# A linear-attention and MoE kernel: decay and bonus rows by the ScalarE queue, and the bonus rows turned ahead of unit 0's transposes

## Chip, cores and metric

One core of a Trainium2 chip. The metric is device time in microseconds of one execution; the median of five runs of the kernel before is 197.82 us (197.74 to 198.13).

## What is computed

The reference is a recurrent attention (RWKV-5 form) followed by a two-layer MLP with a SiLU between its layers. Batch 4, 8 heads, 768 steps, head size 48; the MLP is 384 to 2048 to 384 over all 3072 tokens.

```python
for t in range(S):
    kt, vt, rt = k[:, :, t], v[:, :, t], r[:, :, t]
    cur = np.einsum('bhd,bhe->bhde', u[None] * kt, vt)
    y[:, :, t] = np.einsum('bhd,bhde->bhe', rt, state + cur)
    state = w[None, :, :, None] * state + np.einsum('bhd,bhe->bhde', kt, vt)
...
h = x @ w_in                       # x: y with the heads side by side
out = (h * (1.0 / (1.0 + np.exp(-h)))) @ w_out
```

Two small inputs matter here: `w` (the decay, 8 x 48 numbers) and `u` (the bonus, 8 x 48 numbers).

## The kernel before

The sequence is cut into chunks of 128 steps. A unit is one chunk of one batch element; there are 24, taken chunk by chunk with the four batch elements inside. Unit i has its r, k and v as three loads of 192 KB each on the SP queue (`load`, L64), into six rotating buffers.

In a unit, TensorE transposes r and k of head pairs into PSUM (`p1`, L223), VectorE multiplies them by powers of the decay while it evacuates them (L226 for r, L230 for k), TensorE multiplies them into 128 x 128 score tiles (`p2`, L267 and L269), VectorE masks these (L276), and TensorE multiplies the masked scores with v (`p3y`, L293). The bonus term goes another way: GpSimd computes `ku` = k times u (`nat_ku`, L180) and `rku_f` = r times ku (`nat_rk`, L186), VectorE sums it per head (`bonus_sum`, L197), and ScalarE (unit 0, `bonus_act`, L211) or GpSimd (`bonus_vu`, L203) multiplies v by the sums. VectorE adds the two terms (`p3e`, L300), TensorE transposes the result (`p4`, L346), ScalarE evacuates it (L347), and the MLP's first layer follows (`l1`, L358), later its second (`l2`, L370). From the second chunk on a state is carried as well.

The order of instructions on every engine is the order of the program's text: the schedule is written out by hand from L426 on, and each engine works through its own list in order. MLP matmuls are put between the attention steps as fillers.

What precedes unit 0 is this. `w` and `u` come as rows of four partitions, 1.5 KB each (`load_row`, L84). SP's list starts with the decay row, then r and k of unit 0, the bonus row (handed in as `mid` at L89), v of unit 0, and the loads of units 1 to 3. ScalarE's list starts with a table load and a one-column SiLU (L116). TensorE starts with `spin(5)`, five matmuls on a zeroed tile that serve no result (L125); then `to_cols` turns the decay row into columns (L129), and four more spins follow (L139). From the decay's columns VectorE builds all powers up to 128 in seven doublings (L152 to L156); the tile of the powers is `pif`. Then comes `p1(0)`, with the r transposes, the k transposes, and in between the two evacuations, in the text at L227, the bonus row's turn: `to_cols_u` (L409) transposes it into columns (L129 again), ScalarE copies these (L134), four transposes of the broadcast columns spread them over 128 partitions (`to_rows`, L147), and ScalarE copies that into `u_bc` (L149).

GpSimd's list after its constants begins with a one-column copy that waits for r of unit 1 (`gate`, L434), the issue of the first quarter of the first MLP weight (`win_part(0, 512)`, L417), then `ku` of unit 0, which needs `u_bc`, `rku_f` of unit 0, and the same pair for unit 1, the second quarter's issue, and `vu` of unit 1.

VectorE's list after L230 of unit 0: the two masks of unit 0, L226 and L230 of unit 1, the bonus sums of units 0 and 1 (L197), the two masks of unit 1, and the two additions L300.

```python
    load_row(wrow, w)
    load(0, mid=lambda: load_row(urow, u))
...
    spin(5)
    wT = to_cols(wrow, None)
    spin(4)
...
    p1(0, mid=to_cols_u)
...
    nc.gpsimd.tensor_copy(out=gate, in_=rin[1][:, 0, 0:1])
    win_part(0, 512)
    nat_ku(0)
    nat_rk(0)
```

Of the kernel before, what the change touches and what calls it, by code (L numbers as in the profile page):

```python
# [15 lines left out]
def kernel(  # L16
# [11 lines left out]
    nc = tc.nc  # L28

    B, H, S, D = r.shape  # L30
# [5 lines left out]
    PR = 64 + D  # L36
# [16 lines left out]
    vin = [big.tile([128, H, D], FP, name=f"vin{i}") for i in range(NIN)]  # L53
# [7 lines left out]
    def unit(i):  # L61
        return divmod(i, B)

    def load(i, mid=None):  # L64
        if i >= NU:
            return
        sc, b = unit(i)
        for t, src in ((rin, r), (kin, k), (vin, v)):
            if t is vin and mid:
                mid()  # L70
            nc.sync.dma_start(out=t[i % NIN][:, :, 0:D],
                              in_=src[b, :, sc * C:sc * C + C, :]
                              .rearrange("h t d -> t h d"))
# [4 lines left out]
    urow = cst.tile([NP, 2, 64], FP)  # L78
# [3 lines left out]
        nc.vector.memset(t[:, :, D:64], 1.0)  # L82

    def load_row(t, src):  # L84
        nc.sync.dma_start(out=t[:, :, 0:D], in_=bass.AP(tensor=src.tensor, offset=0,
                                                        ap=[[PW, NP], [D, 2], [1, D]]))

    load_row(wrow, w)
    load(0, mid=lambda: load_row(urow, u))  # L89
    for i in range(1, B):  # L90
        load(i)
    for t in (rin, kin):
        nc.vector.memset(t[0][:, :, D:64], 0.0)
# [6 lines left out]
        out=maskM, in_=maskM, compare_op=ALU.is_ge, fill=0.0,  # L100
# [17 lines left out]
    def spin(n, t=None):  # L118

        if t is None:  # L120
            t = ps.tile([128, 512], FP, name="spin", tag="t", bufs=5)
        else:
            t = t.rearrange("s p t -> s (p t)")
        for _ in range(n):
            nc.tensor.matmul(t, junk[:, 0:128], junk, start=True, stop=True)  # L125

    def to_cols(row, copy):
        t = ps.tile([128, 512], FP, name="cols", tag="t", bufs=5)
        nc.tensor.transpose(t[0:PR, 0:NP], row.rearrange("p j d -> p (j d)")[:, 0:PR],  # L129
                            ident[0:NP, 0:NP])  # L130
        if copy is None:
            return t[0:PR, 0:NP]
        c = cst.tile([PR, NP], FP, name="cols_sb")
        copy(out=c, in_=t[0:PR, 0:NP])  # L134
        return c

    spin(5)
    wT = to_cols(wrow, None)
    spin(4)  # L139
    u_bc = cst.tile([128, H, D], FP)  # L140
    lamC = cst.tile([128, H, D], FP)

    def to_rows(dst, cols):

        t = ps.tile([128, NP, 2, 64], FP, name="rows", tag="t", bufs=5)
        for p in range(NP):
            nc.tensor.transpose(t[:, p, :, :].rearrange("t j d -> t (j d)")[:, 0:PR],  # L147
                                cols(p), ident[0:PR, 0:PR])
        nc.scalar.copy(out=dst.rearrange("t (p j) d -> t p j d", j=2), in_=t[:, :, :, 0:D])  # L149


    nc.vector.tensor_copy(out=pi[:, 0:NP, 1:2], in_=wT.unsqueeze(2))  # L152
# [2 lines left out]
    while n < C:  # L155
        nc.vector.tensor_tensor(  # L156
            out=pi[:, :, 1 + n:1 + 2 * n], in0=pi[:, :, 1:1 + n],
# [14 lines left out]
    def nat_v(i):  # L172
        L = live.setdefault(i, {})
        L["v16"] = wrk.tile([128, H, D], F16, name="v16", bufs=6)
        nc.scalar.copy(out=L["v16"], in_=vin[i % NIN])

    def nat_ku(i):
        L = live.setdefault(i, {})
        L["ku"] = wrk.tile([128, H, D], FP, name="ku")
        nc.gpsimd.tensor_tensor(out=L["ku"], in0=kin[i % NIN][:, :, 0:D], in1=u_bc,  # L180
                                op=ALU.mult)

    def nat_rk(i):
        L = live[i]
        L["rku_f"] = wrk.tile([128, H, D], FP, name="rku_f")
        nc.gpsimd.tensor_tensor(out=L["rku_f"], in0=rin[i % NIN][:, :, 0:D], in1=L["ku"],  # L186
                                op=ALU.mult)
# [23 lines left out]
            nc.scalar.activation(out=L["vu"][:, h, :], in_=vin[i % NIN][:, h, :],  # L211
                                 func=AF.Copy, scale=L["rku"][:, h:h + 1])

    def p1(i, mid=None, spins=0):
        n = i % NIN
        L = live.setdefault(i, {})
        tr = ps.tile([128, NP, C], FP, name="tr", tag="t", bufs=5)
        tk = ps.tile([128, NP, C], FP, name="tk", tag="t", bufs=5)
        spin(spins, tr)
        for t, src in ((tr, rin), (tk, kin)):  # L220
            flat = src[n].rearrange("p h d -> p (h d)")
            for p in range(NP):
                nc.tensor.transpose(t[0:PR, p, :], flat[:, 128 * p:128 * p + PR], ident)  # L223
        rk = wrk.tile([PR, 2, NP, C], FP, name="rk")
        L["rT"] = rk[:, 0]
        nc.vector.tensor_tensor(out=L["rT"], in0=tr[0:PR], in1=lamR, op=ALU.mult)  # L226
        if mid:  # L227
            mid()
        L["kT"] = rk[:, 1]
        nc.vector.tensor_tensor(out=L["kT"], in0=tk[0:PR], in1=lamK, op=ALU.mult)  # L230

# [174 lines left out]
            f()  # L406


    def to_cols_u():  # L409
        t = to_cols(urow, nc.scalar.copy)  # L410
        to_rows(u_bc, lambda p: t[:, p:p + 1].broadcast_to([PR, 128]))

    zero = junk[0:PR, 0:HD].rearrange("r (p c) -> r p c", p=NP)
    gate = cst.tile([128, 1], FP)

    def win_part(c0, c1):
        nc.gpsimd.dma_start(out=win[:, :, c0:c1],  # L417
                            in_=moe_w_in[:, c0:c1].rearrange("(q p) n -> p q n", p=128))
# [4 lines left out]
            in_=moe_w_out[1024 * g:1024 * g + 1024, :].rearrange("(f p) n -> p f n", p=128))  # L423


    p1(0, mid=to_cols_u)  # L426
    nat_v(0)
    lamCT = cst.tile([PR, NP, C], FP)
    for p in range(NP):
# [1 line left out]
                             scale=pi[:, p, C:C + 1])  # L431

    nc.scalar.copy(out=st[0], in_=zero)
    nc.gpsimd.tensor_copy(out=gate, in_=rin[1][:, 0, 0:1])  # L434
    win_part(0, 512)
    nat_ku(0)
    nat_rk(0)
    p2(0)
    p1(1, spins=1)
    bonus_sum(0)  # L440
    nat_ku(1)
    nat_rk(1)
    nat_v(1)
    p3y(0)
    to_rows(lamC, lambda p: lamCT[:, p, :])
    bonus_act(0)
    nc.scalar.copy(out=st[1], in_=zero)
# [8 lines left out]
    spin(1)  # L456
    p4(0)
    p1(2)
    nat_ku(2)
    nat_rk(2)  # L460
    nat_kc(0)
    win_part(1024, 1536)
    win_part(1536, 2048)
    nc.gpsimd.memset(rin[B][:, 0, 0:1], 0.0)
    load(B)
    load(B + 1)
    p4(1)
# [169 lines left out]
```

## Time and profile before

| what | value |
|---|---|
| median of five runs | 197.82 us |
| the profiled execution | 197.77 us |
| its span, first to last instruction | 196.1 us |
| outside the span | 1.7 us |
| TensorE busy | 189.6 us, 97% of the span |
| VectorE, ScalarE, GpSimd busy | 115.4, 90.9, 115.1 us |
| DMA, mean over the span | 123 GB/s |
| wait of L197 for GpSimd in the first 17 us | 0.8 us, once |

A profile has several views. The page gives busy shares and 40 slices of the span; the chain of waits follows the work that ended last back to its start; the timeline lists instructions with start and duration in us, and in brackets how long the engine was idle before and who ended that; the table by stretch gives busy time per engine in chosen windows. Matmul ends in these records are modelled, starts are measured. TensorE is busy nearly throughout, so that what its first useful matmuls wait for early in the span is paid in full, while the other engines' idle time mostly is not.

### The profile page before, as it was taken

To read this page: it belongs to the slowest core of one execution; us is meant where nothing else is said; L and a number is where in the kernel's file an instruction comes from. 1 tells how busy PE (TensorE), PEld (TensorE's weight loads), DVE (VectorE), ACT (ScalarE), POOL (GpSimd) and SP (SyncE) were. 2 spreads that over 40 slices of the span, in tenths; PEclk is the share of its full clock that TensorE was granted. 3 is DMA by queue.
4 is the path that set the end of the run, shared out by engine and by line. 5 is a ranking of instruction groups with operands and counts; after the bars stand their busy time and mean duration, and the time that the engine had idled before them with its cause. 6 is when DMAs were issued, how large, how long until landed. Compare 5 with 4: busy or idle time off the path is not lost.

```text
span 196.1 us, 4923 instructions
## 1 busy us (share of the span) xinstructions
PE 189.6 (97%) x1919; PEld 127.5 (65%) x1919; DVE 115.4 (59%) x233; ACT 90.9 (46%) x207; POOL 115.1 (59%) x145
## 2 busy tenths in 40 slices
PE   7989999999999999999999999999999999999993
PEld 2757878787767887675657656557656556644563
DVE  6687658885857774975486686467576344210121
ACT  3475487799212534216861125682025680069300
POOL 4499969979975779678668737835537710000000
PEclk9999999999999999999999999999999999999999
DMA  4999999999794783477456387616561011210022
GB/s 82 201 191 173 181 230 181 186 193 197 148 201 130 162 175 80 110 172 159 83 104 133 106 181 158 133 32 125 120 162 43 20 22 43 90 51 0 3 82 80
DMA packets 89696, 24.12 MB, mean 123 GB/s; under 512 B 82888, under 2 KB 89672, under 8 KB 89672
## 3 DMA queue, kind: packets, MB, share of 16 engines
q1 hardware_dynamic: 85992, 20.66, 48.7%
q0 software_dynamic: 3680, 3.15, 10.7%
q8 instruction: 15, 0.25, 0.5%
q14 instruction: 9, 0.07, 0.1%
HBM read 20.45 MB, written 4.72 MB: 128 GB/s over the span
## 4 chain that ended last, share of the span: by engine, by line
PE 87%; DVE 4%; issue 4%; POOL 3%; ACT 0%; POOLq 0%; DVEq 0%
PE ops L370 31%; PE hps L358 31%; PE ae L267 11%; PE xs L242 4%; PE y L293 3%; DVE am L276 2%; PE y L290 2%; PE sps L309 2%; PE ops L384 1%; POOL rku_f L186 1%; POOL ku L180 1%; PE yT L346 1%; PE ao L269 1%; DVE y L300 1%; DVE rku L197 1%
## 5 line engine op out<-in xcount | busy, mean ns | idle before, releaser
L361 ACT ACTIVATE gT<-hps 128x256 f16<-128x256 f32 (+1 forms) x128 | 59.7, 493 | 50.6 <-PE hps L358 48.9
L358 PE MATMUL hps<-xT,win 128*128 128x256 f16 (+1 forms) x384 | 69.2, 326 | 0.2
L370 PE MATMUL ops<-wout,gT 128*128 128x384 f16 x368 | 63.8, 326 | 0.0
L358 PEld LDWEIGHTS <-win 128*128 128x128 f16 x384 | 35.4, 98 | 22.9 <-issue 0.8
L370 PEld LDWEIGHTS <-gT 128*128 128x128 f16 x368 | 34.7, 98 | 22.4
L276 DVE TENSOR_TENSOR am<-ae,maskM 128x512 f16<-128x512 f32 x24 | 16.6, 691 | 33.4 <-PE ao L269 33.4
L374 DVE COPY osb<-ops 128x384 f32<-128x384 f32 x23 | 12.7, 553 | 28.8 <-PE ops L370 28.7
L267 PEld LDWEIGHTS ae<-rk 48*128 48x128 f32 x192 | 23.1, 187 | 7.6 <-issue 4.9
L267 PE MATMUL ae<-rk 48*128 48x128 f32 x192 | 27.7, 285 | 0.1
L269 PE MATMUL ao<-rk 48*128 48x128 f32 x192 | 27.7, 285 | 0.0
L203 POOL TENSOR_TENSOR vu<-vin,rku 128x384 f32<-128x384 f32 x23 | 19.1, 830 | 14.3 <-DVE rku L197 14.2
L259 ACT CAST rT<-rk 112x512 f16<-112x512 f32 x20 | 12.3, 615 | 31.7 <-DVE rk L253 31.7
L253 DVE TENSOR_TENSOR rk<-xs,pif 112x512 f32<-112x512 f32 x40 | 25.6, 680 | 1.7 <-PE xs L242 1.7
L180 POOL TENSOR_TENSOR ku<-kin,u_bc 128x384 f32<-128x384 f32 x24 | 24.1, 1006 | 1.9 <-DMA kin<-in_k_dram 1.9
L186 POOL TENSOR_TENSOR rku_f<-rin,ku 128x384 f32<-128x384 f32 x24 | 24.1, 1006 | 1.9
L191 POOL TENSOR_TENSOR kc<-kin,lamC 128x384 f16<-128x384 f32 x24 | 24.0, 1003 | 0.0
L269 PEld LDWEIGHTS ao<-rk 48*128 48x128 f32 x192 | 23.1, 187 | 0.0
L323 POOL CAST stb<-st 112x384 f16<-112x384 f32 x12 | 6.0, 503 | 20.4 <-DVE st L318 20.4
L300 DVE TENSOR_TENSOR y<-y,vu 128x384 f16<-128x384 f32 x24 | 13.4, 557 | 7.6 <-PE y L293 2.2
L276 DVE TENSOR_TENSOR am<-ao,maskM 128x512 f16<-128x512 f32 x24 | 16.3, 680 | 0.0
L197 DVE TENSOR_REDUCE rku<-rku_f 128x8 f32<-128x384 f32 x24 | 13.2, 549 | 2.0 <-POOL rku_f L186 1.6
L325 POOL TENSOR_TENSOR sdec<-st,pif 112x384 f32<-112x384 f32 x16 | 13.3, 836 | 1.1 <-ACT gT L361 1.1
(74 smaller groups left out, 170.0 us busy)
## 6 DMA issues: line engine op xcount, KB each, us to landing
rin<-in_r_dram SPq DMA_DIRECT2D x24, 192.0 KB, 2.8
kin<-in_k_dram SPq DMA_DIRECT2D x24, 192.0 KB, 3.4
vin<-in_v_dram SPq DMA_DIRECT2D x24, 192.0 KB, 3.7
out_dram<-osb SPq DMA_DIRECT2D x23, 192.0 KB, 1.9
win<-in_moe_w_in_dram POOLq DMA_DIRECT2D x4, 384.0 KB, 6.2
wout<-in_moe_w_out_dram POOLq DMA_DIRECT2D x2, 768.0 KB, 9.9
xT<-y SPq DMA_TRANSPOSE x18, 2.3
out_dram<-osh SPq DMA_DIRECT2D x1, 128.0 KB
```

The source lines that it names most:

```text
L180: nc.gpsimd.tensor_tensor(out=L["ku"], in0=kin[i % NIN][:, :, 0:D], in1=u_bc, op=ALU.mult)
L186: nc.gpsimd.tensor_tensor(out=L["rku_f"], in0=rin[i % NIN][:, :, 0:D], in1=L["ku"], op=ALU.mult)
L191: nc.gpsimd.tensor_tensor(out=kc[i % NKC][:, :, 0:D], in0=kin[n][:, :, 0:D], in1=lamC, op=ALU.mult)
L203: nc.gpsimd.tensor_tensor(out=L["vu"], in0=vin[i % NIN], in1=L["rku"].unsqueeze(2).broadcast_to([128, H, D]), op=ALU.mult)
L253: nc.vector.tensor_tensor(out=rk[:, :, :, 64 * g:64 * g + 64], in0=xs[g][0:PR], in1=lam(g), op=ALU.mult)
L267: nc.tensor.matmul(ae[:, p, :], L["kT"][0:D, p, :], L["rT"][0:D, p, :], start=True, stop=True)
L269: nc.tensor.matmul(ao[:, p, :], L["kT"][64:PR, p, :], L["rT"][64:PR, p, :], start=True, stop=True)
L276: nc.vector.tensor_tensor(out=am, in0=a, in1=maskM.unsqueeze(1).broadcast_to([128, NP, C]), op=ALU.mult)
L300: nc.vector.tensor_tensor(out=L["y16"], in0=L["y"], in1=L["vu"], op=ALU.add)
L358: nc.tensor.matmul(hps, win[:, q, ft * 128:(ft + 1) * 128], xts[sc][:, q, b0:b1, :].rearrange("p b t -> p (b t)"), start=(q == 0), stop=(q ...
L361: nc.scalar.activation(out=gts[sc][:, ft, b0 * C:b1 * C], in_=hps, func=AF.Silu)
L370: nc.tensor.matmul(ops, gts[sc][:, ft, b * C:(b + 1) * C], wout[:, ft, :], start=(ft == 0), stop=(ft == NFT - 1))
```

## The change

Three edits in the lead-in, all ahead of unit 0's scores.

- `load_row` issues on ScalarE's queue and no longer on SP's. ScalarE's list starts with the decay row and the bonus row, ahead of the table load. SP's list starts with r of unit 0; its order is otherwise the same.
- TensorE's list: six spins, the decay row's turn, one spin, the bonus row's turn, two spins, the four spreading transposes, and only then r and k of unit 0. There are nine spins as before. ScalarE's copies for the bonus keep their place in ScalarE's order. The argument `mid` goes.
- GpSimd's list: `ku` of unit 0 stands ahead of the gate and of the issue of the first weight quarter.

VectorE's order is unchanged.

```diff
-    def load(i, mid=None):
+    def load(i):
...
         for t, src in ((rin, r), (kin, k), (vin, v)):
-            if t is vin and mid:
-                mid()
             nc.sync.dma_start(out=t[i % NIN][:, :, 0:D],
...
     def load_row(t, src):
-        nc.sync.dma_start(out=t[:, :, 0:D], in_=bass.AP(tensor=src.tensor, offset=0,
+        nc.scalar.dma_start(out=t[:, :, 0:D], in_=bass.AP(tensor=src.tensor, offset=0,
                                                         ap=[[PW, NP], [D, 2], [1, D]]))
 
     load_row(wrow, w)
-    load(0, mid=lambda: load_row(urow, u))
-    for i in range(1, B):
+    load_row(urow, u)
+    for i in range(B):
         load(i)
...
-    spin(5)
+    spin(6)
     wT = to_cols(wrow, None)
-    spin(4)
+    spin(1)
+    ucol = to_cols(urow, nc.scalar.copy)
+    spin(2)
     u_bc = cst.tile([128, H, D], FP)
...
+    to_rows(u_bc, lambda p: ucol[:, p:p + 1].broadcast_to([PR, 128]))
...
-    def p1(i, mid=None, spins=0):
+    def p1(i, spins=0):
...
         nc.vector.tensor_tensor(out=L["rT"], in0=tr[0:PR], in1=lamR, op=ALU.mult)
-        if mid:
-            mid()
...
-    def to_cols_u():
-        t = to_cols(urow, nc.scalar.copy)
-        to_rows(u_bc, lambda p: t[:, p:p + 1].broadcast_to([PR, 128]))
...
-    p1(0, mid=to_cols_u)
+    p1(0)
...
+    nat_ku(0)
     nc.gpsimd.tensor_copy(out=gate, in_=rin[1][:, 0, 0:1])
     win_part(0, 512)
-    nat_ku(0)
     nat_rk(0)
```

## The prediction

> **What bounds the kernel now.** I read the slices of the page first: TensorE's row is full from the fourth slice on (each slice is 4.9 us). Only the lead-in and the last slice have room.
>
> ```profile
> PE   7989999999999999999999999999999999999993
> ...
> DMA  4999999999794783477456387616561011210022
> ```
>
> So an edit to the lead-in is worth what it moves the first filler matmul (hps, L358, at 17.06 us) and little else. Next the chain of waits, cut to the first 20 us, which tells who sets that start:
>
> ```profile
> 8.66 1.02 POOL ku L180
> ...
> 9.75 1.00 POOL rku_f L186
> 10.76 0.96 POOL ku L180
> ...
> 11.80 1.01 POOL rku_f L186
> ...
> 12.84 0.55 DVE rku L197
> 13.39 1.21 DVE am L276 x2
> ...
> 17.06 0.49 PE hps L358 x3
> ```
>
> GpSimd's bonus products of units 0 and 1 run to 12.8 us, VectorE sums unit 1's (L197), and only then masks unit 1's scores (L276). From there masks, y, spin, yT, transposes, yT, ScalarE copy and hps follow without slack. The question is how much that GpSimd wait costs, that is, what is next behind it. The timeline of the first 16 us answers:
>
> ```profile
> 4.08 2.38 DVE L156 TENSOR_TENSOR pif<-pif 112x8 f32<-112x8 f32 x7
> ...
> 5.37 1.06 PE L223 MATMUL tr<-ident,rin 128*112 128x128 f32 x4
> ...
> 6.60 0.69 DVE L226 TENSOR_TENSOR rk<-tr,pif 112x512 f32<-112x512 f32 x1
> ...
> 9.14 0.69 DVE L276 TENSOR_TENSOR am<-ae,maskM 128x512 f16<-128x512 f32 x1 [1.25 <-PE ao L269]
> ...
> 12.84 0.55 DVE L197 TENSOR_REDUCE rku<-rku_f 128x8 f32<-128x384 f32 x1 [0.76 <-POOL rku_f L186]
> 13.31 0.68 DVE L276 TENSOR_TENSOR am<-ae,maskM 128x512 f16<-128x512 f32 x1
> ```
>
> The decay's powers (pif) and r's transposes (tr) end together, at 6.46 and 6.43, and release L226 at 6.60. Unit 1's last score matmul starts at 12.56 and takes 0.27, so it ends at 12.83; the mask of unit 0 began 0.04 after the like end (9.10 to 9.14). Unit 1's mask could thus have begun at 12.87 and began at 13.31. **The wait is worth 0.44 us at most**; behind it stands the chain decay row, powers (pif), L226 and L230 of unit 0, scores, masks, unit 1. VectorE's own order (L226 of unit 1 to the masks of unit 1) has no other gap in it, so whatever delays L226 of unit 0 delays that chain one for one. I call that delay s. The time changes by s - 0.44.
>
> **What the skill says.** "DMA: Bandwidth & Descriptors", section on issuing engines not being separate DMA queues: transfers issued from different engines run on the same 16 engines, and a second issuer only saves issue time. The trace fits: the two row issues hold SP for 0.84 and 0.64 us, and the data are 3 KB. The same page, section on queues, rings and completion order: each engine takes the rings of different queues in turn. No run shows this yet; I use it to bound the bonus row's landing. "TensorE: Matmul & The Clock Gate", section on the clock gate: TensorE starts at half clock and gets the full one after about 3.4 us of sustained work, in a window that runs free. The trace agrees: spins start 427 ns apart up to 5.37 and 216 ns apart at 13 us; transposes go from 213 to 109 ns apart during the k transposes, at about 6.3 us. "ScalarE: Activation LUTs", section on the table load: 1283 ns; the trace has 1.28 us.
>
> **The change, part by part.**
>
> *Rows off SP's queue.* r of unit 0 is issued at 0.81 and not at 1.70, what follows v of unit 0 about 1.5 us earlier. Worth nothing by itself: in the trace r of unit 0 has landed at 4.43 and is used at 5.37, k at 5.49 against 6.22. The later loads (r, k of unit 2 landed at 10.33 and 14.59, used at 15.29 and 15.72; k of unit 3 19.66 against 20.67) only gain slack.
>
> *Rows on ScalarE's queue.* Two issues of 0.84 and 0.64 us from 0.80 end at 2.3; table load 1.28 and SiLU 0.21 behind them end at 3.8 in place of 2.31. ScalarE is next wanted for the columns' copy at 4.96 (below), so 1.1 us of idle time hides it; beyond that each us costs a us. The decay row took 1.97 us from issue to landing (0.81 to 2.78) and should again land near 2.8, wanted at 3.93: hidden. The bonus row, issued near 1.65, takes between 1.97 (nothing beside it) and 2.94 (its time in the trace of before, behind r and k in one ring: 2.80 to 5.74): landed between 3.6 and 4.6. It is wanted at 4.68. I take it as hidden, narrowly.
>
> *Spins and turns.* One more spin ahead of the decay's turn puts it, and pif, 0.43 later: 3.51 to 3.93; pif ends at 6.46 + 0.43 = 6.89. TensorE then: spin at 4.12; bonus turn 0.57 behind that (2.94 to 3.51 was spin to turn before), 4.68; two spins at 4.87 and 5.26; the columns' copy on ScalarE is done by 5.2 (before 0.41 from turn to end of copy), so the spread starts after the spins: 5.69 if its weight load is pulled ahead as that of tr was, 5.83 if there is the gap that the turn had (0.57 against 0.43). Spread transposes have 112 moving columns where tr has 128: warm 96 against 109 ns, so cold 0.213 x 112/128 = 0.187; four make 0.75. r's transposes thus start between 6.44 and 6.58, now at full clock if it is granted at 6.3 again: last start 0.33 later, 0.27 to its end, 7.04 to 7.18. This is later than pif (6.89), so TensorE decides. L226 began 0.14 after its last input before (6.46 to 6.60): 7.18 to 7.32. **s is 0.58 to 0.72; I take 0.65.** k's transposes end 0.44 after r's, at 7.6, before L230 can start (7.25 + 0.61 = 7.86), so k adds nothing. Below, s can't be under 0.43, since pif is bound to six spins; above, see the rivals.
>
> *GpSimd.* The spread ends near 6.65, its copy (0.48) near 7.15; ku of unit 0 starts there and not at 8.66. Gate and weight issue follow (7.59 to 8.64 before, 1.05 in all): issue at 8.3 in place of 7.71, rku_f at 9.3 (before 9.75), ku and rku_f of unit 1 at 10.3 and 11.35, ended at 12.4 in place of 12.8. VectorE wants it after the sum of unit 0, at 11.54 + s + 0.47 = 12.66. **The wait for GpSimd goes entirely.** The weight quarter landed at 14.03 and is used at 17.06: 3 us of cover for 0.6. The gate waited for r of unit 1 (7.53), which now has landed before it is asked.
>
> *What is late next.* Unit 1's scores: 12.87 + 0.65 = 13.52 for the mask, against 13.31. The addition L300 at 14.50 also needs ScalarE's vu of unit 0, which ends at 14.02 + s = 14.67; the masks before it end L300's turn at 14.71, so that only ties.
>
> **Sum.** -0.44 + 0.65 = +0.21 us on the profiled execution's 197.77, which gives 197.98; the median (197.82) is 0.05 higher, so I say 198.0.
>
> **Rivals.**
>
> *The lead pays later.* Loads 0.9 to 1.5 us and GpSimd 0.4 us earlier could close gaps behind 17 us. The table by stretch shows TensorE idle for 0.31 us in 17 to 20 and 0.56 in 35 to 40, about 1.1 between 15 and 40. Against it: those waits are for masks and sums on VectorE, not for loads or GpSimd. If half is closed: 197.98 - 0.55 = 197.4 or below. Chance 0.12.
>
> *The bonus row comes late.* Its turn now stands in TensorE's list ahead of r's and k's transposes, where before only `u_bc` hung on it. From a landing past 4.65 each us costs one. For it: the upper bound is 4.6, and r of unit 0 is issued at the same moment, into the same engines. With its old landing less the 0.64 us of r's earlier start, 5.1, s grows by 0.45: 198.4. Chance 0.18; it would be slower.
>
> *The full clock comes late.* If it is granted after r's transposes (by 7.4), these run at 213 and not 109 ns apart: 0.31 more, and 0.15 at their end, 198.4. If it is granted before 5.5, spread and transposes shrink below pif and s is 0.43: 197.75. The page says the window runs free; no second run shows it. Chance of late 0.15; early lies in the forecast.
>
> The forecast itself: 0.55, between 197.75 and 198.25.
>
> **Chances.** A measurement of this kernel can tell about 0.2%, 0.4 us (below 197.42 or above 198.22). Faster: most of the first rival, 0.10. Slower: the edge of the forecast (0.06) and most of the second and third rivals (0.13 and 0.11), 0.30. Within: 0.60. The range runs from the lower edge with a little of the lead paid, 197.55, to the late row or clock, 198.5; half of the first rival and the worst of the others, under 0.2, are left out.
>
> **What would show it.** In the new trace: no idle time ahead of the sum L197 of unit 1; L226 of unit 0 near 7.25, released by TensorE and not by pif; unit 1's mask released by the scores near 13.5; hps near 17.25; ku of unit 0 near 7.15. Wrong if TensorE stands idle before the bonus turn (late row), if L226 starts near 7.0 (pif decides), or if the first hps is later than 17.3 while the end is not.

## The result, and the profile after

The forecast was 198.0 us, from 197.55 to 198.5. Measured: **199.21 us** (median of 24 executions) against 197.77 us (44 executions of the kernel before). The ratio is 1.0057 with a 95% interval of 1.0038 to 1.0076. (It leaves out four slow executions, those more than 1.5% above the kernel's fastest; the two medians alone give 1.0073.) The change makes the kernel slower, by more than the forecast's range allowed.

The executions after the change do not agree with each other as those before did. The 44 of before lie within 0.95 us. The 24 of after fall into three groups: nine from 197.75 to 198.14, six from 198.97 to 199.37, nine from 200.03 to 200.81. More than a third of them show next to no loss. Any explanation has to account for that too.

The profiled execution took 200.54 us, with a span of 198.8 (before 197.77 and 196.1). The same two rows of the page's slices as shown before:

```profile
PE   6798999989999999999999999999999999999994
...
DMA  6996898999886735656666378436561011220022
```

The slices do not show where the loss arises: TensorE's row is nearly as full as before, since work at half clock counts as busy too, and its last slice is 4 where it was 3. The loss has to be looked for in the timeline of the first 16 us. (Many line numbers have moved, by up to four; r's evacuation is L228 now, the bonus sum L199, `ku` L182.) First the two row transfers and the bonus row's turn:

```profile
0.80 1.25 ACTq L83 DMA_DIRECT2D wrow<-in_w_dram  x1
...
2.09 0.65 ACTq L83 DMA_DIRECT2D urow<-in_u_dram  x1
...
5.39 0.22 PE L127 MATMUL cols<-ident,urow 4*112 4x4 f32 x1 [0.67 <-DVE pif L158]
```

The bonus row is issued at 2.09 and lands at 5.26 by the record of its transfer. TensorE had finished the spin ahead of the turn at 4.72 and stands idle for 0.67 us. The bracket names VectorE (`pif`), which is wrong: the turn doesn't read `pif`, and the only thing that ended just before 5.39 and that the turn needs is the row. (In an experiment below, where the row lands at 5.55, the same bracket names the DMA.) Then what follows on TensorE and VectorE:

```profile
6.37 0.95 PE L147 MATMUL rows<-ident,cols_sb 112*128 112x112 f32 x4
...
7.12 1.06 PE L225 MATMUL tr<-ident,rin 128*112 128x128 f32 x4
...
8.28 0.69 DVE L228 TENSOR_TENSOR rk<-tr,pif 112x512 f32<-112x512 f32 x1 [1.39 <-PE tr L225]
...
11.93 0.69 DVE L276 TENSOR_TENSOR am<-ae,maskM 128x512 f16<-128x512 f32 x1 [2.17 <-PE ao L269]
12.23 1.06 PE L225 MATMUL tr<-ident,rin 128*112 128x128 f32 x4
...
14.54 1.00 DVE L199 TENSOR_REDUCE rku<-rku_f 128x8 f32<-128x384 f32 x2
```

Four transposes that take 1.06 us in all are at half clock; at full clock the same line reads 0.60. Unit 0's transposes and unit 1's r transposes at 12.23 are all at half clock, and so are unit 0's scores between them (213 ns apart). The full clock is granted only at about 13.46: unit 1's k transposes start 213 ns apart at 13.09, 190 at 13.30 and 110 at 13.49. Before the change it came at about 6.3. One thing went as forecast: the bonus sums stand on one line without idle time in front, so the wait for GpSimd is gone.

The chain of waits, cut to the first 20 us, has no GpSimd in it any more. It runs through the turn, the spread, the transposes and the scores on TensorE:

```profile
5.39 0.22 PE cols L127
5.61 0.97 PE spin L123 x2
6.58 0.75 PE rows L147 x4
7.33 0.85 PE tr L225 x4
8.18 0.87 PE tk L225 x4
...
9.07 0.70 DVE rk L230
...
16.07 1.28 DVE am L276 x2
```

**The sum closes on the trace.** L228 of unit 0 begins 1.68 us later than before (6.60 to 8.28). From it to unit 0's mask it takes 3.65 us in place of 2.54: 1.11 more. From that mask to unit 1's it takes 4.12 in place of 4.17, of which 0.44 had been the wait for GpSimd, so 0.39 more. 1.68 + 1.11 + 0.39 - 0.44 = 2.74. The first hps moves from 17.06 to 19.81, 2.75 later, and the span is 2.7 longer. All of the loss arises before 17 us.

### The profile page after: what moved, and what is told of

Its sections match the earlier page's. It is cut to its first block, busy times and chain, and to the rows that moved or that the text cites. A ratio compares the mean times of both kernels' runs of the same rounds, so it can differ in the third digit from the quotient of the medians.

```text
span 198.8 us, 4922 instructions
## 1 busy us (share of the span) xinstructions
PE 191.7 (96%) x1919; PEld 129.6 (65%) x1919; DVE 115.5 (58%) x233; ACT 90.9 (46%) x207; POOL 115.0 (58%) x145
## 3 DMA queue, kind: packets, MB, share of 16 engines
HBM read 20.45 MB, written 4.72 MB: 127 GB/s over the span
## 4 chain that ended last, share of the span: by engine, by line
PE 92%; DVE 5%; issue 1%; ACT 0%; DVEq 0%
PE ops L370 31%; PE hps L358 30%; PE ae L267 13%; PE xs L242 4%; PE y L293 3%; DVE am L276 2%; PE spin L123 2%; PE y L290 2%; PE sps L309 2%; PE ops L384 1%; PE tr L225 1%; PE tk L225 1%; PE ao L269 1%; PE yT L346 1%; PE rows L147 1%
## 5 line engine op out<-in xcount | busy, mean ns | idle before, releaser
L267 PEld LDWEIGHTS ae<-rk 48*128 48x128 f32 x192 | 23.9, 193 | 8.5 <-issue 4.7
L267 PE MATMUL ae<-rk 48*128 48x128 f32 x192 | 28.6, 291 | 0.8 <-DVE rk L230 0.8
L269 PE MATMUL ao<-rk 48*128 48x128 f32 x192 | 28.6, 291 | 0.0
L182 POOL TENSOR_TENSOR ku<-kin,u_bc 128x384 f32<-128x384 f32 x24 | 24.1, 1005 | 6.7 <-ACT u_bc L149 5.2
L259 ACT CAST rT<-rk 112x512 f16<-112x512 f32 x20 | 12.3, 615 | 31.7 <-DVE rk L253 31.7
L269 PEld LDWEIGHTS ao<-rk 48*128 48x128 f32 x192 | 23.9, 193 | 0.0
L199 DVE TENSOR_REDUCE rku<-rku_f 128x8 f32<-128x384 f32 x24 | 13.1, 549 | 1.3 <-POOL rku_f L188 0.8
```

Source lines behind the costliest of these rows:

```text
L267: nc.tensor.matmul(ae[:, p, :], L["kT"][0:D, p, :], L["rT"][0:D, p, :], start=True, stop=True)
L269: nc.tensor.matmul(ao[:, p, :], L["kT"][64:PR, p, :], L["rT"][64:PR, p, :], start=True, stop=True)
```

## The experiments

Three theories were put against each other. **A:** the bonus row lands late, TensorE stands idle just while it has to show work to be given the full clock, and the clock then comes microseconds later. **B:** the new order of TensorE's and GpSimd's work costs by itself. **C:** the late row costs only by its lateness, one for one, and the spread of times follows the landing.

### Rows back on SP's queue, ahead of r

The new order is kept; only the queue is changed, so that both rows come early.

```diff
-        nc.scalar.dma_start(out=t[:, :, 0:D], in_=bass.AP(tensor=src.tensor, offset=0,
+        nc.sync.dma_start(out=t[:, :, 0:D], in_=bass.AP(tensor=src.tensor, offset=0,
```

> The changed kernel with one thing back: both rows are issued by SP again, decay row then bonus row, ahead of r of unit 0. TensorE's, VectorE's and GpSimd's order stay as changed. Theory A (the bonus row lands late, TensorE stands idle for 0.67 us before its turn, and that gap keeps the full clock away for one or two more windows): the bonus row lands near 3.7, no idle time before its turn, full clock near 6.3 us, 197.8 to 198.2 us with little spread. Rival B (the new order of spins and transposes by itself keeps the clock away): a spread up to 200.8 us and a median near 199.2 as in the changed kernel. Rival C (only the serial lateness of the row costs, the clock varies by chance): about 198.0, and the spread stays.

Measured: 197.78 us (197.75 to 198.23, 13 executions), ratio 1.0004 [0.9996, 1.0013].

```profile
4.11 0.61 PE L123 MATMUL spin<-junk 128*128 128x512 f16 x1
4.65 0.21 PE L127 MATMUL cols<-ident,urow 4*112 4x4 f32 x1
...
5.62 0.60 PE L225 MATMUL tr<-ident,rin 128*112 128x128 f32 x4
...
7.04 0.69 DVE L228 TENSOR_TENSOR rk<-tr,pif 112x512 f32<-112x512 f32 x1
```

The bonus row landed at 3.54, its turn ran at 4.65 with no idle time in front, and the full clock came at about 4.65, earlier than theory A had put it (6.3). L228 began at 7.04, unit 1's mask at 13.30 and hps at 17.06; these last two are as before the change. TensorE's list, spins and transposes alike, is that of the changed kernel, so theory B falls: the order itself is neutral. The spread went too, which theory C had not expected. The order is neutral because 0.44 us of wait goes and L228 comes 7.04 - 6.60 = 0.44 later.

### Rows on ScalarE's queue, the rest as before

```diff
-        nc.sync.dma_start(out=t[:, :, 0:D], in_=bass.AP(tensor=src.tensor, offset=0,
+        nc.scalar.dma_start(out=t[:, :, 0:D], in_=bass.AP(tensor=src.tensor, offset=0,
...
-    load(0, mid=lambda: load_row(urow, u))
-    for i in range(1, B):
+    load_row(urow, u)
+    for i in range(B):
```

> The kernel before with only the queue part of the change: both rows are issued by ScalarE, r of unit 0 is SP's first transfer; spins, turns and GpSimd's order as before, so that the bonus row is wanted at 6.8 us only. Theory A: nothing waits for the bonus row, clock near 6.3 us, 197.7 to 198.0 us, little spread; the decay row, landed at 3.46 in the changed kernel and wanted at 3.51, may cost up to 0.1. Rival B: the same. Rival C: the same. If it is slower by over 0.5 us, the queue costs by itself, which none of them says.

Measured: 197.43 us (197.35 to 198.08, 13 executions), ratio 0.9986 [0.9978, 0.9995]. It is faster than both kernels, and than the 197.7 that all three theories gave as the least: none had seen the gain described below. Its timeline:

```profile
6.61 0.19 POOL L434 COPY gate<-rin 128x1 f32<-128x1 f32 x1 [3.87 <-DMA rin<-in_r_dram]
6.66 0.69 DVE L226 TENSOR_TENSOR rk<-tr,pif 112x512 f32<-112x512 f32 x1
...
7.89 0.99 POOL L180 TENSOR_TENSOR ku<-kin,u_bc 128x384 f32<-128x384 f32 x1 [0.22 <-ACT u_bc L149]
...
11.60 1.00 DVE L197 TENSOR_REDUCE rku<-rku_f 128x8 f32<-128x384 f32 x2
...
12.92 0.69 DVE L276 TENSOR_TENSOR am<-ae,maskM 128x512 f16<-128x512 f32 x1 [0.32 <-PE ao L269]
```

With the rows gone from SP's list, r of unit 1 lands at 6.56 and no longer at 7.53. GpSimd's gate opens a us earlier, the weight issue is done before `u_bc` is ready at 7.80, and `ku` starts at 7.89 in place of 8.66. The sums no longer wait, and unit 1's mask is 0.39 earlier. The bonus row lands late here too (5.04), but its turn stands behind unit 0's transposes and wants it at 6.22.

### The changed kernel with two more spins in front of the bonus turn

The row stays as late as in the changed kernel. TensorE is given something to do meanwhile.

```diff
-    spin(1)
+    spin(3)
     ucol = to_cols(urow, nc.scalar.copy)
```

> The changed kernel with two more spins between the decay row's and the bonus row's turn (three for one), so that TensorE is busy until 5.4 us while the bonus row is as late as it was. Theory A: no gap, clock near 6.3 us; the spread's transposes start near 6.5 and run warm, L228 near 7.7, that is 1.1 us later than before, less the 0.44 of the wait that goes: about 198.4, between 198.0 and 198.7, with little spread. Rival B: as the changed kernel, 199.2 with the spread. Rival C: not faster than the changed kernel, 199.2 or 0.1 more.

Measured: 197.88 us (197.75 to 198.57, 14 executions), ratio 1.0011 [1.0002, 1.0019].

```profile
4.12 1.12 PE L123 MATMUL spin<-junk 128*128 128x512 f16 x3
...
5.38 0.18 PE L127 MATMUL cols<-ident,urow 4*112 4x4 f32 x1
...
6.32 0.60 PE L225 MATMUL tr<-ident,rin 128*112 128x128 f32 x4
...
7.03 0.69 DVE L228 TENSOR_TENSOR rk<-tr,pif 112x512 f32<-112x512 f32 x1
```

This is the run that decides between A and C. The row landed at 5.24 and the turn ran at 5.38, within 0.02 us of the changed kernel's, yet the transposes take 0.60 and L228 begins at 7.03 instead of 8.28. The full clock was there from 4.77, which is why the time came out below A's range: A had put the clock at 6.3 and L228 at 7.7. None of the 14 executions is over 198.57; of the changed kernel's 24, fifteen are at 198.97 or more. What costs is the idle time on TensorE, through the clock, not the lateness of the row. Theory C falls.

### The new order, with the rows on SP in the order of before

```diff
     load_row(wrow, w)
-    load_row(urow, u)
-    for i in range(B):
+    load(0, mid=lambda: load_row(urow, u))
+    for i in range(1, B):
```

(With it, `load_row` issues on SP and `load` has its argument `mid` again.)

> The changed kernel with both rows on SP's queue in the order of before (decay row, r, k, bonus row, v of unit 0): only the order on TensorE and GpSimd is changed. The bonus row landed at 5.74 before, so the gap before its turn grows from 0.67 to about 1.2 us. Theory A: the clock is late at least as often as in the changed kernel, median 199.2 to 201. Rival B: 199.2, as the changed kernel. Rival C: 0.5 us over the changed kernel's fast runs, 198.3, up to 199.7.

Measured: 198.50 us (198.07 to 199.74, 9 executions: five from 198.07 to 198.5, four from 199.51 to 199.74), ratio 1.0056 [1.0033, 1.0079]. The profile is of an execution of 198.07, in which the full clock was there by the turn at 5.68 or just after it, as the transposes behind it take 0.60:

```profile
5.68 0.19 PE L129 MATMUL cols<-ident,urow 4*112 4x4 f32 x1 [0.96 <-DMA urow<-in_u_dram]
```

Here L228's like begins at 7.33, that is 0.29 later than with the rows early on SP, and hps at 17.36, 0.30 later: a row that lands at 5.55 costs 0.3 us by its lateness alone, with the clock there. The median of the second group is 1.4 us above that of the first, as with the first two groups of the changed kernel. This is a half miss for A: a longer gap should have given at least as many late executions as in the changed kernel, and some above 200. There were four of nine, and none above 200. Theory C's time (198.3, up to 199.7) fits this run at least as well; what speaks against C is the run with more spins and the four profiles below.

### The kernel before with only GpSimd's reordering

```diff
+    nat_ku(0)
     nc.gpsimd.tensor_copy(out=gate, in_=rin[1][:, 0, 0:1])
     win_part(0, 512)
-    nat_ku(0)
```

> The kernel before with only GpSimd's order changed: ku of unit 0 ahead of the gate and the first weight issue, while the bonus row is still turned after unit 0's transposes. Theory A: u_bc is there at 8.4 as before, so ku of unit 0 starts at 8.45, gate and issue follow it, and rku_f of unit 1 ends near 13.6 in place of 12.8; the mask of unit 1 moves from 13.31 to about 14.1: 198.5 us, between 198.3 and 198.7, no long tail, since TensorE has no new gap ahead of the clock. Rival B and C say the same of the time. If it is 197.8, the order on GpSimd is worth nothing in this place.

Measured: 198.35 us (198.05 to 198.94, 10 executions), ratio 1.0035 [1.0023, 1.0047].

```profile
13.24 0.55 DVE L197 TENSOR_REDUCE rku<-rku_f 128x8 f32<-128x384 f32 x1 [1.15 <-POOL rku_f L186]
```

Without an earlier `u_bc`, `ku` starts at 8.12, the gate and the weight issue follow it instead of preceding it, and everything behind is later: the wait grows from 0.76 to 1.15, unit 1's mask comes at 13.71. The reordering pays only beside an early spread.

### The kernel before with both rows issued first, on two queues

```diff
-    load_row(wrow, w)
-    load(0, mid=lambda: load_row(urow, u))
-    for i in range(1, B):
+    load_row(wrow, w, nc.sync)
+    load_row(urow, u, nc.scalar)
+    for i in range(B):
...
-    spin(5)
+    spin(4)
...
-    nc.gpsimd.tensor_copy(out=gate, in_=rin[1][:, 0, 0:1])
+    nc.gpsimd.tensor_copy(out=gate, in_=vin[0][:, 0, 0:1])
```

(`load_row` takes the issuing engine as a third argument here.)

> A version meant to beat both: the decay row stays SP's first transfer, the bonus row alone goes to ScalarE's queue and is turned after unit 0's transposes as before; four spins and not five ahead of the decay's turn (its row lands at 2.78); the gate on GpSimd waits for v of unit 0 and not for r of unit 1. Theory A: no gap in TensorE's lead-in; the chain from the decay row starts 0.43 earlier, the GpSimd chain 0.3 to 0.8 earlier, so unit 1's mask starts at about 12.45 in place of 13.31: 196.9 us, between 196.7 and 197.3. If the wait for GpSimd is not gone, 197.3 to 197.5. Rivals B and C: the same.

Measured: 197.54 us (197.07 to 198.19, 21 executions), ratio 0.9984 [0.9975, 0.9993]. A gain, but about a third of the one expected. With both queues issuing at 0.81, the bonus row landed at 2.74 and the decay row only at 3.22 (2.78 alone), so that TensorE waited 0.20 for it, and v of unit 0, which opens the gate here, landed only at 6.93. L197 still waits 0.65 for GpSimd. What was gained is L226 at 6.42 and unit 1's mask at 13.02.

### The kernel before without spins

This makes the clock late on purpose, with every row on time.

```diff
-    spin(5)
     wT = to_cols(wrow, None)
-    spin(4)
```

> The kernel before without its nine spins ahead of unit 0's transposes: TensorE stands idle until the decay row (2.8 us) and again until r of unit 0 (4.4 us), nothing comes later than before by any transfer. Theory A: the decay chain is 0.6 us earlier, but the full clock is granted only after 8 us, often after 11: scores and transposes of units 0 and 1 run at half clock, 198 to 200 us with a spread of over 1 us. Rival C (idle time does not move the clock): the earlier chain gives 197.3 to 197.8, no spread. Rival B (transposes in place of spins keep the clock away) goes with theory A here.

Measured: 199.22 us (198.76 to 199.78, 6 executions), ratio 1.0076 [1.0058, 1.0094].

```profile
6.05 0.69 DVE L224 TENSOR_TENSOR rk<-tr,pif 112x512 f32<-112x512 f32 x1
...
14.52 0.69 DVE L274 TENSOR_TENSOR am<-ae,maskM 128x512 f16<-128x512 f32 x1 [0.58 <-PE ao L267]
```

Unit 0 is ready for VectorE 0.55 us earlier than before, because TensorE's list is shorter, and yet unit 1's mask is 1.21 later. TensorE stayed at half clock until 12.3. A late clock is worth at least this much here, without any late row. The run does not tell what made it late: the idle time, or that spins count for more towards the clock than the transposes left in the list. For the changed kernel the run with the rows early on SP tells: its list is the same, and only the gap is gone.

### The changed kernel again, three times

Nothing is edited; these are three more profiles, to see whether the time follows the landing of the row or the clock.

> The changed kernel once more, for a further profile. Theory A: the bonus row lands near 5.2 and the gap before its turn is 0.5 to 0.7 us in every execution; what differs is when the full clock is granted. If before the gap ends (under 5.4 us): about 197.8 to 198.1 us. If near 9 us: about 199.2. If past 11 us: 200 to 200.8. Rival C: the landing of the row differs between executions by as much as the time does, with the clock granted at the same time in all.

> As the run before: the same kernel a third time. Theory A: same landing and gap, total time by the time of the grant: under 5.4 us 197.8 to 198.1, near 9 us 199.2, past 11 us 200 to 200.8. Rival C: the landing differs with the total.

> As the two runs before: the same kernel a fourth time. Theory A: same landing and gap, total time by the time of the grant: under 5.4 us 197.8 to 198.1, near 9 us 199.2, past 11 us 200 to 200.8. Rival C: the landing differs with the total.

| execution | bonus row landed | gap before its turn | full clock from about | L228 of unit 0 | unit 1's mask | time |
|---|---|---|---|---|---|---|
| third profile | 5.09 | 0.73 | 4.03 | 7.01 | 13.28 | 197.76 |
| second profile | 5.35 | 0.77 | 8.65 | 8.37 | 14.65 | 199.14 |
| first profile | 5.26 | 0.67 | 13.46 | 8.28 | 16.05 | 200.54 |
| fourth profile | 5.32 | 0.74 | 13.84 | 8.35 | 16.28 | 200.76 |

From the timelines of the third and the fourth profile:

```profile
5.23 0.18 PE L127 MATMUL cols<-ident,urow 4*112 4x4 f32 x1 [0.73 <-DVE pif L158]
...
6.17 0.60 PE L225 MATMUL tr<-ident,rin 128*112 128x128 f32 x4
```

```profile
5.46 0.22 PE L127 MATMUL cols<-ident,urow 4*112 4x4 f32 x1 [0.74 <-DVE pif L158]
...
7.19 1.06 PE L225 MATMUL tr<-ident,rin 128*112 128x128 f32 x4
```

The row lands within 0.26 us in all four and the gap is the same within 0.1, while the time differs by 3.0 us and follows the clock in order. Where the clock came before the gap opened (4.03), the gap costs nothing that can be seen. Each of the three groups of times has its own moment of the clock in these profiles: about 4, about 8.7, and 13.5 to 13.8. The times are those that theory A had set down for such moments, within 0.1 us.

In the late executions TensorE stands idle a second time, for 0.78 us, until L230 has the k half of unit 0 ready for the scores. In the first profile:

```profile
9.82 0.58 PE L267 MATMUL ae<-rk 48*128 48x128 f32 x1 [0.78 <-DVE rk L230]
```

The kernel before has no idle time there, as the bonus row's turn and spread filled it. In the second profile the clock had come by then (8.65); in the first and the fourth it came 3.6 and 4.0 us after this stretch. Whether the second gap kept the clock away once more, no run tests.

## Why the prediction was wrong

**The wait for GpSimd: right.** It was priced at 0.44 us and went. With rows early on SP the time changed by 0.44 - 0.44 = 0, with the queue alone by 0.06 - 0.44 = -0.38 at unit 1's mask (L226 at 6.66 in place of 6.60) and -0.34 in the measured median. That VectorE passes a delay of L226 on one for one held in both.

**The order's own cost: right in kind, a little high.** s was put at 0.65, with TensorE deciding. In the three profiles where the clock came early and the row by 5.24 (rows early on SP, more spins, the third of the changed kernel) it was 0.41 to 0.44, about what `pif` behind the sixth spin allows, which is the lower bound that the prediction gave.

**"Rows on ScalarE's queue": the step that failed first.** It read: "landed between 3.6 and 4.6. It is wanted at 4.68. I take it as hidden, narrowly." Each of its terms was low. The first issue took 1.25 us on ScalarE and not the 0.84 that it had taken on SP; the bonus row was thus issued at 2.09 and not 1.65; and it took 3.17 us and not 2.94 at most, beside r and k on the other queue. Landed: 5.26. TensorE standing idle before the turn is the sign of failure that the prediction had named. The rival with the late row had this mechanism; that its landing of 5.1 came near is in part luck, since its sum (the old landing less 0.64) has neither the slower issue nor the longer way in it.

**The price of the late row: the larger error.** The prediction charged a late row one for one (0.45) and a late clock separately (0.46), as two rivals that exclude each other. They are one chain: the row's gap falls into the time in which TensorE has to earn the clock. The extra spins show it, since they leave the row late and give the time back. And a late clock was priced at r's transposes alone, "0.31 more, and 0.15 at their end", as if it came by 7.4 at the latest. It came at 8.65 to 13.84, and where it came past 13, unit 0's scores (1.11 us in the profiled execution) and unit 1's transposes (0.39) pay as well.

The lateness by itself cost next to nothing: with the row landed at 5.09 (third profile) or 5.24 (more spins), L228 began at 7.01 and 7.03, as with the rows early (7.04), because `pif` is not there sooner. It cost 0.3 only where the row landed at 5.55. The loss of the first profile is therefore the clock's: L228 at 8.28 and not 7.01, 1.27, then 1.11 and 0.39, 2.77 in all; the two executions differ by 200.54 - 197.76 = 2.78.

**"Worth nothing by itself", of the rows leaving SP's queue: wrong.** Whoever asks only when r of unit 0 is used finds no gain. The gain is at r of unit 1, which GpSimd's gate waits for: landed 0.97 earlier, it took the weight issue out of the way of `ku`. That is worth 0.34 us of the 0.44 that the change was after. In the changed kernel it bought nothing, because `ku` had been moved ahead of the gate.

**How the clock came.** The Trainium skill, "TensorE: Matmul & The Clock Gate", section on why this matters for kernels, warns of idle gaps over some 3 us. That is about losing a clock already granted, in mid-kernel. Here a gap of 0.67 to 0.77 before the first grant went with a late clock in three profiles of four. The same page's section on the clock gate says that the window runs free, which would fit times that fall into groups, and puts the warm-up at under 1% of a typical span. Between the fastest and the slowest of the four profiles above the moment of the grant made 3.0 us of 198, or 1.5%. And where the prediction says that the trace agrees with a grant after about 3.4 us of work, it does so only loosely: before the change the first spin starts at 1.26 and the clock came at about 6.3, 5.0 us later.

**Still open.** How much idle time delays the grant, whether the second gap matters, and why the grant falls at different moments in executions that are alike, no run here settles. The rows in before's order gave a longer gap (0.96) and fewer late executions than the changed kernel; nine executions are too few to say whether that is chance. That the gap is what makes the clock late in this order is shown by its absence in the runs with early rows and with more spins (27 executions, none over 198.57); that it doesn't do so always, by the third profile.

## What to carry to other kernels

While TensorE is still earning its full clock, an idle gap is not priced by its length: 0.7 us cost up to 3.0 here. So before moving work that waits for a transfer to the front of TensorE's list, compare its landing, not its issue, with the moment it is wanted, and if the margin is no larger than your doubt about the landing (here 0.1 us of margin, and a landing 0.66 past the latest estimate) put spins in front or leave it behind work that is ready. When times of a kernel spread into groups, take several profiles and line them up by clock before looking for a cost in the code. And when a transfer leaves a queue, follow all that stands behind it to whoever waits there, gates included.

## What was not expected of the hardware

- The first issue of a row took 0.84 us on SP, and 1.25 us on ScalarE with SP issuing at the same moment. Whether ScalarE's is longer by itself or because of SP's, no run separates; SP's was not slowed (0.85 in the run with one row on each queue). There the decay row landed at 3.22, though, and not at 2.78.
- A row of 1.5 KB landed 1.97 us after its issue as SP's first transfer, and 3.17 us after it as ScalarE's second, while 192 KB loads ran on SP's queue.
- The full clock came at about 4.0, 8.65, 13.46 or 13.84 us in four executions of one program whose timelines agree within 0.2 us up to the gap.
- The column of the granted clock in the table by stretch reads 1.00 all through the first 15 us of the profiled execution, though TensorE was at half clock until 13.46; only the spacing of the matmuls (213 against 109 ns for a transpose) shows it.
